# Attention feeding a routed expert layer: logits in a scores' bank, the second routing round drawn forward and partly on GpSimd, expert 0's rows and weights in another order, loads three steps ahead

## The chip, the cores and the metric

The kernel runs on one core of a Trainium2 chip. The metric is the device time of one execution in microseconds (us). Five engines work beside each other, each with its own instruction queue, taken in order: TensorE (PE in the profile; its weight loads are PEld), VectorE (DVE), ScalarE (ACT), GpSimd (POOL) and SyncE (SP), which here issues the plain DMAs. GpSimd issues the indirect ones (gathers and scatters of rows).

## The reference

First a recurrent attention over 4 batches, 8 heads, 768 positions, head size 64; then a layer of 8 experts in which each of the 3072 rows goes to one expert only.

```python
state = gamma[None, :, None, None] * state + einsum('bhd,bhe->bhde', k[:, :, t], v[:, :, t])
y[:, :, t] = scale * einsum('bhd,bhde->bhe', q[:, :, t], state)      # for t in range(768)
x = y.transpose(0, 2, 1, 3).reshape(3072, 512)
logits = x @ w_gate                                                   # 512 x 8
expert_idx = argmax(logits, axis=1)
gate_w = softmax(logits)[arange(3072), expert_idx]
for e in range(8):                                                    # rows sorted by expert
    y_sorted[lo:hi] = maximum(x_sorted[lo:hi] @ w1[e], 0.0) @ w2[e]   # 512x1024, 1024x512
out = gate_w[:, None] * y_sorted[inv_perm]
```

## The kernel before

**Attention** runs in 12 steps (`STEPS`), each a block of 128 positions of two batches and all 8 heads. The recurrence is done in chunks: inside a block by scores (`scores`, L520) under a causal mask (`am`, DVE, L522) and their product with v (`within`, L569); between blocks by a state of 64x64 per head (`with_state` L540, `next_state` L553). k, v and q lie in DRAM with 64 numbers (256 bytes) to a row, q in pieces of two rows. `load` issues them on SP two steps ahead of their use; `scale_q` and `scale_v` multiply by decay factors on GpSimd (L477, L482); `turn_k` and `turn_q` transpose through PE and copy back on ACT (L488, L507, L501).

`within` leaves the block of x transposed in `x[s]`. One step later `logits` (L598) multiplies it by the gate's weights `wg` into the PSUM tile `parts`, ACT copies that to `lgT` (L601), `logits_of` turns it into the PSUM tile `lgp` (L607), and DVE reduces that into `lg` (L608). `to_rows` (DVE, L582) and `store` (SP, L589) write the same block as rows into the DRAM tensor `x_d`.

PSUM has 8 banks: four under the tag `sc` (scores, transposes of q), two under `tr` (transposes of k, state update, `parts`, `lgp`, the routing's small products), two under `y`.

**Routing** (`place`) is a generator, so that its pieces can be put between pieces of the attention. It runs in three rounds over steps 0 to 4, 5 to 8 and 9 to 11 (`NEXT = (0, 5, 9, 12)`). A round finds each row's expert and gate, the row's rank in its expert (`rk`, PE), the pieces of the gate in bf16 (`told`), a one-hot of places (`val`) and of ranks (`here`), multiplies the two (`found`, PE, L687) and adds the result to the table `inv` (L691). After the second round the first 256 rows of experts 0 and 1 are known, and four gathers on GpSimd (L169) fetch them from `x_d` into `xs2`. The places of the pieces in a step are written out by hand in `WHEN`: a letter stands for a point of the step (p, a, b, c), each letter takes the generator to its next `yield`.

**After the last step** the early rows of expert 0, copied from `xs2` to `xe` (DVE, L803), are transposed (`tre`, L821) and copied to `xTa`. Layer 1 of expert 0 on these 256 rows (`layer1`, L226, eight blocks `f`) runs while the third round of the routing is made. Then come the gathers of the later rows, sums and differences of blocks of w2 and of hidden values (`halves_of_w` L268, `halves_of_h` L256 to L259), and `pair` (L352), which makes layer 2 of 256 rows by seven block products instead of eight. The rest of expert 0 and experts 1 to 7 follow in a loop over experts. The weights of expert 0 are loaded within the last steps of the attention (L153 w1, L158 w2), 2 MB each; those of expert 1 need buffers that are free only once the attention's buffers are given up.

From `tc.manual_schedule` on, every engine takes its instructions in the order of the program text. This is true of SP too: a store that waits for DVE holds up the loads behind it.

Of the kernel before, what the change touches and what calls it, by code (L numbers as in the profile page):

```python
# [53 lines left out]
def kernel(  # L54
# [93 lines left out]
    w1v = w1.rearrange("e (dt p) f -> p e dt f", p=P)  # L148
    w2v = w2.rearrange("e (ft p) d -> p e ft d", p=P)

    def weights1(pool, e):
        w1t = pool.tile([P, 1, DT, F], F32, tag="w1t", name="w1t")
        nc.sync.dma_start(w1t, w1v[:, ds(e, 1), :, :])  # L153
        return w1t

    def weights2(pool, e):
# [282 lines left out]
    with ExitStack() as actx:  # L439
# [19 lines left out]
        def load(nm, s, b, parts=1):  # L459
            m, b1, e = where[s]  # L460
            src = {"q": q, "k": k, "v": v}[nm]
            if nm == "q":
                to = att.tile([P, H, 2 * D], F32, tag=nm, name=nm, bufs=3)
                for part in (ts(i, H // parts) for i in range(parts)):
                    nc.sync.dma_start(to[:, part, :], src[2 * b1 + b, part, ts(m, 2 * P), :].rearrange(
                        "h (t e) d -> t h (e d)", e=2))
            else:
                to = att.tile([P, H, D], F32, tag=nm, name=nm, bufs=6)
                nc.sync.dma_start(to, src[2 * b1 + b, :, ts(2 * m + e, P), :].rearrange("h t d -> t h d"))
            raw[nm, s, b] = to  # L470

# [120 lines left out]
        early = []  # L592

        def logits(s):
            parts = ps("tr", 2, "parts")[:, 0 : 2 * P]
            m = P // DT
            for dt in range(DT):
                nc.tensor.matmul(parts[ts(dt, m), :], lhsT=wg[:, dt, :], start=True, stop=True,  # L598
                                 rhs=x[s][:, dt, :, :].rearrange("p b t -> p (b t)"))
            lgT = att.tile([P, 2 * P], F32, tag="lgT", name="lgT", bufs=1)  # L600
            nc.scalar.copy(out=lgT, in_=parts)  # L601
            return lgT

        def logits_of(s, lgT):
            tr = ps("tr", 2, "lgp")[:, 0 : 2 * P].rearrange("p (b t) -> p b t", b=2)
            for b in range(2):
                nc.tensor.transpose(tr[:, b, :], lgT[:, ts(b, P)], ident)  # L607
            return lambda: nc.vector.tensor_reduce(  # L608
                lg[:, 2 * s : 2 * s + 2, :], tr.rearrange("p b (a e) -> p b e a", a=DT)[:, :, 0:E, :], axis=AX.X,
                op=ALU.add)  # L610
# [3 lines left out]
        def place(i):  # L614
# [20 lines left out]
            nc.vector.tensor_reduce(gate, ex, axis=AX.X, op=ALU.add)  # L635
            nc.vector.tensor_scalar(out=gate, in0=gate, scalar1=1e-9, scalar2=None, op0=ALU.add)
            nc.vector.reciprocal(gate, gate)
            yield
            rk = ps("tr", 2, "rk")[:, 0 : n * E].rearrange("p (b e) -> p b e", e=E)
            nc.tensor.matmul(rk, lhsT=before, rhs=oh, start=True, stop=False)  # L640
# [12 lines left out]
            if i == 0:  # L653
# [5 lines left out]
            nc.vector.tensor_tensor(out=at, in0=inner(oh, TC), op=ALU.mult, in1=bass.AP(  # L659
                tensor=is_col.tensor, offset=is_col.offset,  # L660
                ap=[list(is_col.ap[0]), list(is_col.ap[1]), [0, E], list(is_col.ap[2])]))
            if i < NR - 1:
                yield
            part = gate
            for j in range(2, 5):
                nc.vector.tensor_copy(told[:, mine, j], part)
                if j < 4:
                    less = att.tile([P, MOST_T], F32, tag="less", name="less", bufs=2)[:, 0:n]
                    nc.vector.tensor_tensor(out=less, in0=part, in1=told[:, mine, j], op=ALU.subtract)
                    part = less  # L670
            if i < NR - 1:
# [8 lines left out]
            here = small("here", P, dt=BF16)  # L680
            for b in range(n):
                nc.vector.tensor_scalar(out=here[:, b, :], in0=rrow, scalar1=prow[:, b : b + 1], scalar2=None,
                                        op0=ALU.is_equal)
            yield
            found = ps("tr", 2, "found")[:, 0 : 5 * E * TC]
            for b in range(n):
# [31 lines left out]
        load_all("k", 1)  # L718
        load_all("v", 1)
        load("q", 2, 0)  # L720
        ctx.enter_context(tc.manual_schedule(engines={PE, ACT, POOL, DVE, SP}))
        nc.sync.dma_start(wg[:, :, 0:E], w_gate.rearrange("(dt p) e -> p dt e", p=P))
        xTa = first.tile([P, DT, EARLY], F32, tag="xTa", name="xTa")
# [11 lines left out]
        am.append(scores(0, 1))  # L735
        xe = keep.tile([P, HALF, DM], F32, tag="xe", name="xe")
        rest = iter(())
        WHEN = {5: "abc", 6: "ab", 7: "ab", 8: "pa", 9: "ac", 10: "ab", 11: "pa"}

        def step(s, at):  # L740
            if at in WHEN.get(s, ""):
                next(rest, None)

        for s in range(STEPS):
            if s + 2 < STEPS:
                if s % 2 == 0:
                    load("q", s + 2, 1)
                load_all("k", s + 2)
                load_all("v", s + 2)
                if s % 2 and s + 3 < STEPS:  # L750
                    load("q", s + 3, 0)
            if s % 2 and s + 1 < STEPS:
                scale_q(s + 1, 1)
# [12 lines left out]

            def ahead():
                for b in range(2):
                    turn_k(s + 1, b)

            def ahead_q():
                if s % 2:
                    for b in range(2):
                        turn_q(s + 1, b)

            if s:
                lgT = logits(s - 1)
                if s + 1 < STEPS:
                    ahead()
                reduce = logits_of(s - 1, lgT)  # L780
# [16 lines left out]
                if s + 1 < STEPS:  # L797
                    step(s, "a")
            next_state(s)
            step(s, "b")  # L800
            if s + 1 == STEPS:
                for t in range(HALF):
                    nc.vector.tensor_copy(xe[:, t, :].rearrange("p (a q l) -> p q a l", q=Q, l=L),  # L803
                                          xs2[0][:, t, :].rearrange("p (q a l) -> p q a l", q=Q, l=L))
# [9 lines left out]
        we = [att.tile([P, FH * DH], F32, tag=tag, name="we", bufs=bufs)  # L814
              for tag, bufs in (("q", 3), ("q", 3), ("q", 3), ("qs", 2))]
# [29 lines left out]
        S = halves_of_h(hTa, [att.tile([P, FH * P], F32, tag="k", name="he", bufs=6) for _ in range(4)], nc.gpsimd)  # L845
        which = regs(0)

        late = turns(xs2[0], xTa, range(HALF, TC))
# [1 line left out]
        def some(n):  # L850
            for _ in range(n):
                next(late)

        pair(hTa, wa[1], S, T, oa, egates, lambda: fetch_ahead(which, 0),
             lambda name: att.tile([P, FH * P], F32, tag="v", name=name, bufs=6)[:, 0:DH], some,
             (("sc", 4), ("sc", 4), ("y", 2), ("y", 2)))
        scatter(oa, targets(*early, "_e"), range(HALF))
        turn(xs2[1], xT1, range(TC))
# [208 lines left out]
```

## Time and profile before

| what | us |
|---|---|
| median of 3 runs | 471.01 (470.87 to 472.51) |
| the profiled execution, its own time | 471.93 |
| its span, first to last instruction | 470.2 |
| PE busy | 437.0 (93% of the span) |
| DVE busy | 283.9 (60%) |
| GpSimd busy | 245.3 (52%) |
| ACT busy | 127.1 (27%) |
| mean granted TensorE clock | 0.976 |

The attention takes up about the first 120 us of the span, the early rows of expert 0 run to 168 us, the loop over experts takes the rest. The page cuts the span into 40 slices of 11.75 us; a digit is the busy share of a slice in tenths. In the row of the clock a 9 is full speed. In a timeline row the first number is the start, the second the time, and the bracket says how long the engine had been idle and who ended it. In the chain of waits each row is a piece of the path that ended last.

### The profile page before, as it was taken

How to read it: one execution, taken by the hardware profiler on the slowest of the kernel's cores; microseconds unless marked ns; L12 is line 12 of the kernel's file. 1: busy time of each engine (PE TensorE's matmuls, PEld its weight loads, DVE VectorE, ACT ScalarE, POOL GpSimd, SP SyncE). 2: the span in 40 equal slices, each digit the busy share in tenths (PEclk: the TensorE clock that was granted, in tenths of full speed). 3: DMA queues.
4: the chain of work that ended last, by engine and by line, in shares of the span. 5: the costliest groups of instructions: out<-in, count | busy, mean ns of one | idle time of the engine just before them, and what ended most of it. 6: DMA issues, size and time to landing. Idle time of an engine off the chain costs nothing.

```text
span 470.2 us, 9505 instructions
## 1 busy us (share of the span) xinstructions
PE 437.0 (93%) x3595; PEld 355.7 (76%) x3595; DVE 283.9 (60%) x597; ACT 127.1 (27%) x283; POOL 245.3 (52%) x192
## 2 busy tenths in 40 slices
PE   7799989999389799999999999999999999999992
PEld 5678877887277594557996896799799689689772
DVE  4444578769347795762676477568856768754410
ACT  2354444463111020221231123123213212212310
POOL 4565426431302336918851983688198369369311
PEclk9999999999769899999999999999999999999997
DMA  9999989999820049904815360462453416001001
GB/s 203 207 227 241 204 187 255 238 211 310 288 45 18 24 157 393 372 10 183 256 55 182 90 234 4 181 219 100 184 199 116 172 36 231 5 6 62 4 28 49
DMA packets 93927, 72.75 MB, mean 155 GB/s; under 512 B 53866, under 2 KB 78442, under 8 KB 93808
## 3 DMA queue, kind: packets, MB, share of 16 engines
q1 hardware_dynamic: 88544, 58.74, 44.4%
q0 software_dynamic: 5120, 12.60, 7.5%
q8 instruction: 47, 0.77, 0.7%
q14 instruction: 72, 0.59, 0.4%
q10 hardware_dynamic: 144, 0.05, 0.0%
HBM read 60.88 MB, written 14.68 MB: 161 GB/s over the span
## 4 chain that ended last, share of the span: by engine, by line
PE 78%; DMA 6%; DVE 6%; issue 5%; ACT 2%; SPq 1%; POOL 1%; POOLq 0%; ACTq 0%; DVEq 0%
PE p L306 24%; PE p L352 16%; PE p L239 12%; PE p L226 6%; PE sc L520 3%; PE y L569 3%; PE hp L226 3%; PE yp L352 3%; DMA k<-in_k_dram 3%; PE trq L488 2%; PE new L553 2%; ACT kT L507 1%; DMA q<-in_q_dram 1%; PE y L540 1%; DMA xs<-x_d,src_e 1%
## 5 line engine op out<-in xcount | busy, mean ns | idle before, releaser
L239 PE MATMUL p<-w2t,hT 128*8 128x128 f32 (+6 forms) x496 | 66.4, 360 | 0.0
L239 PEld LDWEIGHTS p<-w2t,hT 128*8 128x8 f32 (+6 forms) x496 | 32.6, 123 | 29.5 <-issue 26.8
L212 DVE STREAM_TRANSPOSE xT<-xs 32x512 f32<-32x512 f32 x64 | 44.9, 702 | 6.0 <-issue 4.9
L169 POOL DMA_INDIRECT xs<-x_d,src x28 | 29.3, 1046 | 35.1 <-DVE gate_e L204 23.8
L397 POOL DMA_INDIRECT out_dram<-o,dst x30 | 29.8, 995 | 27.9 <-ACT o L247 11.3
L482 POOL TENSOR_TENSOR vs<-v,dec 128x512 f32<-128x512 f32 x23 | 24.1, 1064 | 35.6 <-DMA v<-in_v_dram 29.7
L522 DVE TENSOR_TENSOR am<-sc,causal 128x512 f32<-128x512 f32 x48 | 29.9, 684 | 19.5 <-PE sc L520 19.4
L212 DVE STREAM_TRANSPOSE xTs<-xs 32x512 f32<-32x512 f32 x48 | 33.7, 702 | 12.7 <-issue 11.9
L1026 POOL COPY turn_of<-t 128x1 f32<-128x1 f32 x6 | 1.1, 182 | 72.5 <-DVE t L292 72.5
L352 PE MATMUL p<-ws,hs 128*128 128x256 f32 x168 | 37.4, 379 | 0.0
L306 PE MATMUL p<-t,s 128*128 128x196 f32 (+5 forms) x192 | 35.8, 329 | 0.0
L306 PE MATMUL p<-t,w1t 128*128 128x196 f32 (+5 forms) x192 | 35.8, 329 | 0.0
L352 PEld LDWEIGHTS p<-ws,hs 128*128 128x128 f32 x168 | 31.9, 190 | 4.3
L310 DVE TENSOR_TENSOR hT<-p,q 128x196 f32<-128x196 f32 (+5 forms) x72 | 24.8, 361 | 15.7 <-PE p L306 15.2
L268 POOL TENSOR_TENSOR ws<-w2t,ws 128x1024 f32<-128x1024 f32 x14 | 33.5, 2391 | 0.6
L268 POOL TENSOR_TENSOR ws<-w2t 128x1024 f32<-128x1024 f32 x14 | 33.1, 2367 | 0.1
L477 POOL TENSOR_TENSOR qs<-q,dec 128x512 f32<-128x512 f32 x22 | 22.6, 1050 | 20.2 <-DMA q<-in_q_dram 17.4
L306 PEld LDWEIGHTS p<-t,s 128*128 128x128 f32 x192 | 32.4, 190 | 0.0
L306 PEld LDWEIGHTS p<-t,w1t 128*128 128x128 f32 x192 | 32.4, 190 | 0.0
L358 DVE SCALAR_TENSOR_TENSOR o<-p,gate,q 128x256 f32<-128x256 f32 x21 | 10.0, 483 | 29.5 <-PE p L352 29.1
L310 DVE TENSOR_TENSOR q<-p,q 128x196 f32<-128x196 f32 (+5 forms) x48 | 16.5, 360 | 17.9 <-PE p L306 12.9
L352 PE MATMUL p<-w2t,hT 128*128 128x256 f32 x112 | 27.0, 382 | 0.2 <-ACT q L367 0.2
(204 smaller groups left out, 828.3 us busy)
## 6 DMA issues: line engine op xcount, KB each, us to landing
w1t<-in_moe_w_dram SPq DMA_DIRECT2D x8, 2048.0 KB, 9.1
w2t<-in_moe_w_dram SPq DMA_DIRECT2D x8, 2048.0 KB, 11.2
k<-in_k_dram SPq DMA_DIRECT2D x24, 256.0 KB, 5.3
v<-in_v_dram SPq DMA_DIRECT2D x24, 256.0 KB, 5.5
x_d<-xg SPq DMA_DIRECT2D x48, 128.0 KB, 3.8
q<-in_q_dram SPq DMA_DIRECT2D x11, 512.0 KB, 6.0
q<-in_q_dram SPq DMA_DIRECT2D x2, 256.0 KB, 3.5
out_dram<-o,dst POOLq DMA_INDIRECT x30, 3.1
```

The lines of the kernel that those rows point to most:

```text
L169: nc.gpsimd.indirect_dma_start(out=xs[:, t, :], out_offset=None, in_=x_d[0:rows, :], in_offset=bass.IndirectOffsetOnAxis(ap=idx[:, t : t + ...
L212: nc.vector.transpose(xT[ts(g, L), :, 0 : n * P].rearrange("p a (t r i) -> p r t a i", r=Q, i=L)[:, r, :, :, :], xs[ts(r, L), tiles[0] : t ...
L226: nc.tensor.matmul(hp, lhsT=w1t[:, 0, dt, ts(f, P)], rhs=xT[:, dt, 0:n], start=(dt == 0), stop=(dt == DT - 1))
L239: nc.tensor.matmul(y[j * z : j * z + m, 0:c], lhsT=hT[:, f, t * P + r0 : t * P + r0 + m], rhs=w2t[:, 0, f, ts(j, c)], start=(i == 0), stop ...
L268: by.tensor_tensor(out=ws[i], in0=sums[i][0], in1=sums[i][1], op=ALU.subtract)
L306: nc.tensor.matmul(rows(y), lhsT=a(d, f), rhs=b(d), start=start and d == 0, stop=d == 1, skip_group_check=True)
L310: nc.vector.tensor_tensor(out=to, in0=rows(y), in1=rows(plus), op=ALU.add)
L352: nc.tensor.matmul(y, lhsT=a[:, f, :], rhs=b[:, f, :], start=start and f == 0, stop=f == FH - 1, skip_group_check=True)
L397: done = nc.gpsimd.indirect_dma_start(out=out[:, :], out_offset=bass.IndirectOffsetOnAxis(ap=idx[:, t : t + 1], axis=0), in_=o[:, t, :], i ...
L477: by.tensor_tensor(out=qs[:, e, part, :], in0=got[:, part, ts(e, D)], op=ALU.mult, in1=inner(dec[:, ts(2 * where[s][0] + e, H)][:, part], D))
L482: by.tensor_tensor(out=vs, in0=raw.pop(("v", s, b)), op=ALU.mult, in1=inner(dec[:, ts(NC + 2 * where[s][0] + where[s][2], H)], D))
L522: nc.vector.tensor_tensor(out=am[j], in0=sc[j], in1=middle(causal[:, :], HP), op=ALU.mult)
```

## The change

- `logits` and `logits_of` share one bank of the tag `sc`, in place of two tiles of the tag `tr`.
- Loads run three steps ahead: k, v and both q of step 2 are issued before the small load of `wg`, k and v have 8 buffers for 6, q has 4 for 3.
- In the second and third round the pieces of the gate (`tell`) and the one-hot of ranks (`find`) go to GpSimd. The second round is put in fewer and earlier pieces: at points a and the new r (ahead of `within`) of step 9, and twice at p of step 10. Point p moves ahead of `logits`.
- The copies to `xe` come after `within` of the last step, one on DVE and one on ACT; `pad_ranks` moves into step 10.
- w1 of expert 0 is loaded as two halves, still in step 9; w2 in step 11, after that step's store; the store of step 10 no longer stands behind both.
- After the last step the logits are finished ahead of layer 1, and the third round is cut at `f` 1 and 4 (before: 0, 2 and 5). The third of the four `halves_of_w` goes to GpSimd.

```diff
-    def weights1(pool, e):
+    def weights1(pool, e, parts=1):
-        nc.sync.dma_start(w1t, w1v[:, ds(e, 1), :, :])
+        for part in (ts(i, F // parts) for i in range(parts)):
+            nc.sync.dma_start(w1t[:, :, :, part], w1v[:, ds(e, 1), :, part])
...
         def logits(s):
-            parts = ps("tr", 2, "parts")[:, 0 : 2 * P]
+            bank = ps("sc", 4, "parts")
+            parts = bank[:, 0 : 2 * P]
...
-        def logits_of(s, lgT):
-            tr = ps("tr", 2, "lgp")[:, 0 : 2 * P].rearrange("p (b t) -> p b t", b=2)
+        def logits_of(s, lgT, bank):
+            tr = bank[:, 2 * P : 4 * P].rearrange("p (b t) -> p b t", b=2)
...
             nc.vector.reciprocal(gate, gate)
+            by = nc.gpsimd if i else nc.vector
+            def tell():
+                part = gate
+                for j in range(2, 5):
+                    by.tensor_copy(told[:, mine, j], part)
+                    if j < 4:
+                        less = att.tile([P, MOST_T], F32, tag="less", name="less", bufs=2)[:, 0:n]
+                        by.tensor_tensor(out=less, in0=part, in1=told[:, mine, j], op=ALU.subtract)
+                        part = less
+            if i:
+                tell()
             yield
...
-            if i < NR - 1:
+            here = small("here", P, dt=BF16)
+            def find():
+                for b in range(n):
+                    by.tensor_scalar(out=here[:, b, :], in0=rrow, scalar1=prow[:, b : b + 1], scalar2=None,
+                                     op0=ALU.is_equal)
+            if i:
+                find()
+            else:
                 yield
...
         load("q", 2, 0)
+        load("q", 2, 1)
+        load_all("k", 2)
+        load_all("v", 2)
         ctx.enter_context(tc.manual_schedule(engines={PE, ACT, POOL, DVE, SP}))
         nc.sync.dma_start(wg[:, :, 0:E], w_gate.rearrange("(dt p) e -> p dt e", p=P))
...
-        WHEN = {5: "abc", 6: "ab", 7: "ab", 8: "pa", 9: "ac", 10: "ab", 11: "pa"}
+        WHEN = {5: "abc", 6: "ab", 7: "ab", 8: "pa", 9: "ar", 10: "pp"}
...
-            if s + 2 < STEPS:
-                if s % 2 == 0:
-                    load("q", s + 2, 1)
-                load_all("k", s + 2)
-                load_all("v", s + 2)
-                if s % 2 and s + 3 < STEPS:
-                    load("q", s + 3, 0)
+            if s + 3 < STEPS:
+                if s % 2:
+                    load_all("q", s + 3)
+                load_all("k", s + 3)
+                load_all("v", s + 3)
...
+            step(s, "p")
             if s:
-                lgT = logits(s - 1)
+                logit = logits(s - 1)
...
-                step(s, "p")
-                if s + 1 == STEPS:
-                    step(s, "a")
                 to_rows(s - 1)
                 reduce()
-                if s - 1 != NEXT[NR - 1]:
-                    store(s - 1)
+                store(s - 1)
                 if s == NEXT[NR - 1]:
-                    wa = [weights1(first, 0)]
-                if s == NEXT[NR - 1] + 1:
+                    wa = [weights1(first, 0, 2)]
+                if s + 1 == STEPS:
                     wa.append(weights2(first, 0))
-                    store(s - 1)
...
             step(s, "b")
-            if s + 1 == STEPS:
-                for t in range(HALF):
-                    nc.vector.tensor_copy(xe[:, t, :]..., xs2[0][:, t, :]...)
+            if s == NEXT[NR - 1] + 1:
+                pad_ranks(acc[:, NR - 1, 0:2])
+            step(s, "r")
             within(s, y, am)
...
+        for t in range(HALF):
+            copy = nc.scalar.copy if t else nc.vector.tensor_copy
+            copy(out=xe[:, t, :]..., in_=xs2[0][:, t, :]...)
-        lgT = logits(STEPS - 1)
+        logit = logits(STEPS - 1)
         rest = place(NR - 1)
-        pad_ranks(acc[:, NR - 1, 0:2])
...
+        logits_of(STEPS - 1, *logit)()
+        next(rest)
         to_rows(STEPS - 1)
         store(STEPS - 1)
         for f in range(FT):
             layer1(EARLY, xTa, wa[0], hTa, f, (("sc", 4),))
-            if f == 0:
-                logits_of(STEPS - 1, lgT)()
-                next(rest)
-            if f == 2:
+            if f == 1:
                 next(rest)
                 ne = count()
-            if f == 5:
+            if f == 4:
                 next(rest)
                 next(rest, None)
...
-        T = halves_of_w(wa[1], we)
+        halves_of_w(wa[1], we, [0, 1])
+        halves_of_w(wa[1], we, [2], nc.gpsimd)
+        T = halves_of_w(wa[1], we, [3])
```

More of the change, by code (lines that the diff above doesn't have):

```diff
@@ L462, in load @@
             if nm == "q":
-                to = att.tile([P, H, 2 * D], F32, tag=nm, name=nm, bufs=3)
+                to = att.tile([P, H, 2 * D], F32, tag=nm, name=nm, bufs=4)
                 for part in (ts(i, H // parts) for i in range(parts)):
@@ L467, in load @@
             else:
-                to = att.tile([P, H, D], F32, tag=nm, name=nm, bufs=6)
+                to = att.tile([P, H, D], F32, tag=nm, name=nm, bufs=8)
                 nc.sync.dma_start(to, src[2 * b1 + b, :, ts(2 * m + e, P), :].rearrange("h t d -> t h d"))
@@ L601, in logits @@
             nc.scalar.copy(out=lgT, in_=parts)
-            return lgT
-        def logits_of(s, lgT):
-            tr = ps("tr", 2, "lgp")[:, 0 : 2 * P].rearrange("p (b t) -> p b t", b=2)
+            return lgT, bank
+        def logits_of(s, lgT, bank):
+            tr = bank[:, 2 * P : 4 * P].rearrange("p (b t) -> p b t", b=2)
             for b in range(2):
@@ L661, in place @@
                 ap=[list(is_col.ap[0]), list(is_col.ap[1]), [0, E], list(is_col.ap[2])]))
-            if i < NR - 1:
-                yield
[L664 to L671, printed above, removed]
+            here = small("here", P, dt=BF16)
[6 more added lines that the diff above has]
+            else:
+                yield
+                tell()
                 yield
@@ L679, in place @@
                 yield
[L680 to L683, printed above, removed]
+                find()
             yield
@@ L737 @@
         rest = iter(())
-        WHEN = {5: "abc", 6: "ab", 7: "ab", 8: "pa", 9: "ac", 10: "ab", 11: "pa"}
+        WHEN = {5: "abc", 6: "ab", 7: "ab", 8: "pa", 9: "ar", 10: "pp"}
         def step(s, at):
-            if at in WHEN.get(s, ""):
+            for _ in range(WHEN.get(s, "").count(at)):
                 next(rest, None)
         for s in range(STEPS):
-            if s + 2 < STEPS:
-                if s % 2 == 0:
-                    load("q", s + 2, 1)
-                load_all("k", s + 2)
-                load_all("v", s + 2)
-                if s % 2 and s + 3 < STEPS:
-                    load("q", s + 3, 0)
+            if s + 3 < STEPS:
[3 more added lines that the diff above has]
+                load_all("v", s + 3)
             if s % 2 and s + 1 < STEPS:
@@ L774, in ahead_q @@
                         turn_q(s + 1, b)
+            step(s, "p")
             if s:
-                lgT = logits(s - 1)
+                logit = logits(s - 1)
                 if s + 1 < STEPS:
                     ahead()
-                reduce = logits_of(s - 1, lgT)
+                reduce = logits_of(s - 1, *logit)
                 if s + 1 < STEPS:
                     ahead_q()
-                step(s, "p")
-                if s + 1 == STEPS:
-                    step(s, "a")
                 to_rows(s - 1)
                 reduce()
-                if s - 1 != NEXT[NR - 1]:
-                    store(s - 1)
+                store(s - 1)
                 if s == NEXT[NR - 1]:
-                    wa = [weights1(first, 0)]
-                if s == NEXT[NR - 1] + 1:
+                    wa = [weights1(first, 0, 2)]
+                if s + 1 == STEPS:
                     wa.append(weights2(first, 0))
-                    store(s - 1)
                 if s in NEXT:
                     rest = chain(rest, place(NEXT.index(s) - 1))
-                if s + 1 < STEPS:
-                    step(s, "a")
+                step(s, "a")
             next_state(s)
             step(s, "b")
-            if s + 1 == STEPS:
-                for t in range(HALF):
-                    nc.vector.tensor_copy(xe[:, t, :].rearrange("p (a q l) -> p q a l", q=Q, l=L),
-                                          xs2[0][:, t, :].rearrange("p (q a l) -> p q a l", q=Q, l=L))
+            if s == NEXT[NR - 1] + 1:
+                pad_ranks(acc[:, NR - 1, 0:2])
+            step(s, "r")
             within(s, y, am)
@@ L808 @@
             step(s, "c")
-        lgT = logits(STEPS - 1)
+        for t in range(HALF):
+            copy = nc.scalar.copy if t else nc.vector.tensor_copy
+            copy(out=xe[:, t, :].rearrange("p (a q l) -> p q a l", q=Q, l=L),
+                 in_=xs2[0][:, t, :].rearrange("p (q a l) -> p q a l", q=Q, l=L))
+        logit = logits(STEPS - 1)
         rest = place(NR - 1)
-        pad_ranks(acc[:, NR - 1, 0:2])
         oa = xs2[0][:, 0:HALF, :]
         we = [att.tile([P, FH * DH], F32, tag=tag, name="we", bufs=bufs)
-              for tag, bufs in (("q", 3), ("q", 3), ("q", 3), ("qs", 2))]
+              for tag, bufs in [("q", 4)] * 4]
         for t in range(HALF):
@@ L843 @@
         arm, over = arms(ne)
-        T = halves_of_w(wa[1], we)
-        S = halves_of_h(hTa, [att.tile([P, FH * P], F32, tag="k", name="he", bufs=6) for _ in range(4)], nc.gpsimd)
+        halves_of_w(wa[1], we, [0, 1])
+        halves_of_w(wa[1], we, [2], nc.gpsimd)
+        T = halves_of_w(wa[1], we, [3])
+        S = halves_of_h(hTa, [att.tile([P, FH * P], F32, tag="k", name="he", bufs=8) for _ in range(4)], nc.gpsimd)
         which = regs(0)
@@ L854 @@
         pair(hTa, wa[1], S, T, oa, egates, lambda: fetch_ahead(which, 0),
-             lambda name: att.tile([P, FH * P], F32, tag="v", name=name, bufs=6)[:, 0:DH], some,
+             lambda name: att.tile([P, FH * P], F32, tag="v", name=name, bufs=8)[:, 0:DH], some,
              (("sc", 4), ("sc", 4), ("y", 2), ("y", 2)))
```

## The prediction

> **What bounds the kernel now.** I read the slices first, then the chain of waits where PE has a hole, then the timeline there. PE is busy in nine tenths of nearly every slice, so the time is PE's work plus PE's holes.
>
> ```profile
> PE   7799989999389799999999999999999999999992
> PEclk9999999999769899999999999999999999999997
> DMA  9999989999820049904815360462453416001001
> ```
>
> The holes are in slices 0, 1, 10, 11 and 13; the granted clock falls with the big one. Its chain of waits (start, us, what):
>
> ```profile
> 121.18 5.62 DMA xs<-x_d,src_e
> 126.83 0.43 DVE xe L803
> 127.28 0.69 DVE xT L575
> 128.02 1.07 PE parts L598 x4
> ```
>
> PE stands from 120.64 to 128.02, 7.4 us. It waits for a copy of x (L575) that has nothing to do with the gathers; in DVE's queue it stands behind the copies to `xe`, and those wait for rows gathered late, since the second round's result came at 119.4. A second hole stands ahead of `pair`, timeline of PE and POOL:
>
> ```profile
> 150.83 1.96 PE L352 MATMUL yp<-w2t,hTa 128*128 128x256 f32 x8 [0.29 <-issue]
> 156.20 7.27 PE L352 MATMUL yp<-we,he 128*128 128x256 f32 x24 [3.40 <-DVE he L257]
> 156.20 1.26 POOL L258 TENSOR_TENSOR he<-hTa,he 128x512 f32<-128x512 f32 x1 [1.74 <-DVE he L257]
> 157.43 1.26 POOL L259 TENSOR_TENSOR he<-hTa 128x512 f32<-128x512 f32 x1
> ```
>
> The third place is small now and matters for what follows, SP and PE in steps 0 and 1:
>
> ```profile
> 14.37 1.04 SPq L722 DMA_DIRECT2D wg<-in_moe_w_gate_dram  x1
> 15.50 2.62 SPq L465 DMA_DIRECT2D q<-in_q_dram  x1
> 18.17 2.11 SPq L469 DMA_DIRECT2D k<-in_k_dram  x2
> 20.32 2.91 SPq L469 DMA_DIRECT2D v<-in_v_dram  x2
> 21.65 0.64 PE L598 MATMUL parts<-xT,wg 128*32 128x256 f32 x8
> 23.67 0.63 PE L488 MATMUL trk<-ident,k 128*128 128x128 f32 x4 [1.38 <-DMA k<-in_k_dram]
> 24.84 0.63 PE L488 MATMUL trk<-ident,k 128*128 128x128 f32 x4 [0.54 <-DMA k<-in_k_dram]
> ```
>
> The gate's weights `wg` are issued ahead of step 2's loads; the first `parts` needs them at 21.65. From 26 to 120 us PE's idle sums to 4.1 us outside the big hole: the attention there is bound by PE, although the DMA engines are at nine tenths too.
>
> **What the Trainium skill says.** "TensorE: Matmul & The Clock Gate", Part 1: the clock is halved after an idle window of some 3.4 us and restored after a busy one. The trace agrees: 0.50 from 123.3 to 136.9 after the 7.4 us hole, and again from 157.4 to 160.8 after 3.4 us of idleness. "DMA: Bandwidth & Descriptors", Queues, rings and completion order: each DMA engine consumes a ring's descriptors in order. The trace agrees: `wg`, 16 KB, took 6.4 us from issue to landing, behind what was issued before it. "SBUF — State Buffer", two separate sides: GpSimd and a VectorE instruction with two SBUF inputs or in a two-port mode lock each other out for a whole instruction. The trace agrees: while POOL scaled v (62.68 to 64.72) two small DVE steps took 0.80 and 0.93 us where their neighbours take 0.24.
>
> ```profile
> 62.68 2.04 POOL L482 TENSOR_TENSOR vs<-v,dec 128x512 f32<-128x512 f32 x2 [2.64 <-DMA v<-in_v_dram]
> 63.02 0.80 DVE L626 TENSOR_TENSOR dl<-lg,mx 128x80 f32<-128x80 f32 x1
> 63.85 0.93 DVE L628 TENSOR_SCALAR top<-dl 128x80 f32<-128x80 f32 x1
> 64.82 0.24 DVE L629 TENSOR_TENSOR top<-top,em 128x80 f32<-128x80 f32 x1
> ```
>
> **The change part by part**, on the clock of the profile before; shifts are summed at the end.
>
> *Loads further ahead.* q, k and v of step 2 (four k/v loads and one q, 1.57 MB) now stand before `wg`. Their issues took from 15.50 to 23.23, 7.7 us, so `wg` is issued at 22.1 instead of 14.37. Landing: it landed at 14.37 + 6.4 = 20.8; q and k then passed in 4.1 us (the last k at 24.84), v needs another 2.4 (two loads at the 1.2 between the two k): 27.2. Issue plus 6.4 gives 28.5. I take 27.6. PE is in order, so the transposes of k and q behind `parts` wait too. With `parts` 0.6 and the k transposes 1.2, `lgp` starts at 29.4 instead of 25.30: +4.1 (bounds: 0 if `wg` overtakes, 5.0). PE is idle for 5.9 us, so I expect half clock when it resumes: one or two windows of 3.4 us, in which half the work gets done, 1.7 to 3.4 lost, up to 6 if transposes don't count as activity; I take 3.0 (bounds 0 and 6). Early loss 7.1. In return k of step 6 is in time: −1.25 (PE's wait at 60.35). POOL's waits for v (29.7 us in 9) end too, worth nothing, since PE hardly ever waits for POOL there.
>
> *Logits in a scores' bank.* In each step `lgp` starts 0.12 us after the last k transpose (a `tr` bank is still being copied), and the state update 0.27 to 0.41 late in four even steps: together about 2.6. With three tiles a step in `tr` for five this goes; I take −2.2. The new wait is `parts` for the first `am`: in step 2 that ends near 32.07, `parts` starts at 32.17; nothing, by a hair (worst 0.1 a step). The fourth q transpose needs a bank too, one is copied by then.
>
> *Second round.* `rk` (0.4) moves ahead of `within` in step 9; the one-hot it reads was ready at 102.93, PE is there at 102.1: +0.9, and `within` is queued behind it. `found` moves ahead of `logits` in steps 8 and 10 and holds a `tr` bank, so the second k transpose waits for one copy: +0.6. On POOL: `find`, 8 instructions of 128 elements. The nearest row is an affine select of 128 (0.28); a memset of 128 takes 0.19, a two-input 512 takes 1.05. I take 0.30, 2.4 in all, from 105.2, and `val` (1.48) shares the lock: 109.1, while PE is there at 108.5 or a bit later: +0.3. `tell`, 5 small ones of some 0.2, is hidden. The four gathers follow at about 112 (0.3 + 1.0 each, behind two scalings of v), when w1, issued near 107, is almost in; the first two land by 119, needed at 121.
>
> *After the last step.* The copy L575 no longer waits: PE goes on at 120.9 with `parts`, transposes from 121.4 (1.2 at full clock, 1.97 before), `lgp` 0.45, the copy to `xTa` to 123.25. Layer 1 starts at 123.3 instead of 132.10: −8.8. Layer 1 to `pair`: before 150.83 − 132.10 = 18.7, of which 2.3 lost to the half clock and 0.45 `lgp`; after 8 x 1.72 + `rk` 0.35 + wait and count 1.1 + `found` 0.6 = 15.9: −2.8. POOL's 6 `find` (1.8) and DVE's `val` (1.16) end near 131.6, `found` is due at 133.5. Then `src` at 135.5, gates and arms to 137.3, three `halves_of_w` on DVE (1.23 each) to 141.0, the two sums L256, L257. On POOL four gathers until 141.2, then the third `halves_of_w`, 2.37 by its L268 rows, against DVE in the same lock, then 2 x 1.26: the third product can start at 147.4, and five products of 1.72 end at 156.1. From the start of `pair` (139.2) that is 16.9, before 168.48 − 150.83 = 17.65; a half-clock window in it costs about what it did. I take −0.3 (bounds −2.1 and +1.0). w2 is issued near 121, lands in some 11, used at 137; w1's second DMA costs SP one more 0.47 issue. From `pair` on everything is relative to its end, expert 1's loads too.
>
> **Sum**: 4.1 + 3.0 − 1.25 − 2.2 + 1.8 − 8.8 − 2.8 − 0.3 = −6.45. The span 470.2 becomes 463.8. The profiled execution took 471.93, 1.7 more than its span and 0.9 more than the median 471.01; off the median: 464.5.
>
> **Rivals.** (1) *The early stall is cheap*: `wg` lands early or the clock stays up or returns at once (−3 to −5), and `pair` goes without the lock (−1.8). For it: a stall of 1.9 us at the same place cost no clock. Against: 5.9 is longer than 3.4. 457.5. (2) *It is dear*: two more half-clock windows (+3), `found` late by one; 468. (3) *The copies still wait*: gathers took 6.1 us to land beside the weights; if the same congestion meets them, PE waits some 3 at 121: 467.5. (4) *Slower*: `find` on POOL. Each us of its price costs 8 at the first `found` and 6 at the second. Past 0.3, time is lost as 14 x (price − 0.3) less a slack of 2.2 at the second; the gain is gone at about 0.9 and past 1.1 the kernel is measurably slower; at 1.3 it takes 476.3. Against: no one-input row of POOL of this size is above 0.28.
>
> **How the numbers follow.** Forecast 0.55, (1) 0.27, (2) 0.09, (3) 0.05, (4) 0.04. The forecast's own range is 461 to 467.5. 80% takes in nearly all of (1) and most of (2): 456 to 469. A difference within 0.5% (2.35 us) is about what a measurement of this kernel can't tell from none; faster is under 468.65: 0.54 + 0.27 and parts of (2) and (3), 0.86; same 0.09; slower 0.05.
>
> **What would show it.** Right: PE's wait for L575 gone, gathers of `src_e` near 112 plus the shift, a wait of PE at the first `parts` for `wg` of about 6 us with the clock at half after it, no PE wait for k later, layer 1 of `xTa` near 127. Wrong: no wait for `wg`; `tre` waiting for `xe`; `found` waiting for `here`; the loop over experts of another length than 302 us (from 168.5 to the end).

## The result, and the profile after

The changed kernel takes 469.31 us (median of 20 runs, 467.27 to 471.92), beside 472.00 for the kernel before on the same chip (20 runs, 469.73 to 476.66). The ratio is **0.9941 [0.9919, 0.9962]**: 2.8 us faster, where 6.5 were forecast. Its profiled execution took 469.96 us over a span of 468.2; mean clock 0.978.

The three rows of slices, now 11.7 us each (busy tenths of PE, granted clock, DMA):

```profile
PE   7779999998887999999999999999989999999992
PEclk9979999998999799999999999999999999999998
DMA  8999999996671079705804441380472416001001
```

The slice of 3 (the tenth, counted from 0) is gone from PE's row, and slices 9 to 12 show a long shallow dent of 8 and 7 in its place. The clock falls in slice 2 (23 to 35 us: after the wait for `wg`), a little in slice 9 (105 to 117: step 10) and in slice 13 (from 152: `pair`). The chain of waits where PE stood for 7.4 us before, and now stands for 0.84:

```profile
124.82 1.92 PE y L570 x32
...
126.76 0.59 ACT xT L578
...
127.38 0.69 DVE xT L576
...
128.11 0.63 PE parts L600 x4
128.74 1.04 PE tre L833 x8
...
130.44 2.64 PE hp L227 x11
```

What is left is a chain of two copies of x^T, on ACT and then on DVE. Layer 1 starts at 130.44 (132.10 before). The timeline of SP and PE where `wg` now stands behind the loads of step 2:

```profile
20.11 2.53 SPq L470 DMA_DIRECT2D v<-in_v_dram  x2
22.75 1.00 SPq L739 DMA_DIRECT2D wg<-in_moe_w_gate_dram  x1
26.60 1.08 PE L600 MATMUL parts<-xT,wg 128*32 128x256 f32 x8 [4.63 <-DMA wg<-in_moe_w_gate_dram]
27.61 1.97 PE L489 MATMUL trk<-ident,k 128*128 128x128 f32 x8
```

`wg` is issued at 22.75 instead of 14.37, PE waits 4.63 us for it and goes on at half clock: `parts` takes 1.08 instead of 0.64, the transposes 1.97 instead of 1.09. No wait for k follows. The timeline of DVE, POOL and PE in step 10 is the new one:

```profile
105.77 0.19 DVE L672 TENSOR_SCALAR prow<-ranks 128x8 int32<-128x8 int32 x1
106.28 0.33 POOL L645 CAST told<-less 128x8 bf16<-128x8 f32 x1
106.58 5.65 POOL L681 TENSOR_SCALAR here<-rrow,prow 128x128 bf16<-128x128 bf16 x8
106.65 1.64 DVE L692 TENSOR_TENSOR val<-at,told 128x1280 bf16<-128x1280 f32 x1
108.73 0.33 PE L701 MATMUL found<-val,here 128*128 128x160 bf16 x2
109.39 0.24 PE L701 MATMUL found<-val,here 128*128 128x160 bf16 x1 [0.34 <-POOL here L681]
...
112.29 0.24 PE L701 MATMUL found<-val,here 128*128 128x160 bf16 x1 [0.34 <-POOL here L681]
112.46 0.64 PE L600 MATMUL parts<-xT,wg 128*32 128x256 f32 x8
```

PE takes one product of `found` each 0.58 us, as POOL hands out one row of the one-hot after another, from 108.73 to 112.46: 3.73 us for work of 0.7. The first of the eight lasts 1.57, beside `val` on DVE (1.64 here, 1.48 before); the rest come 0.58 apart. By windows, the time after it (columns: PE busy, PEld, DVE, ACT, POOL, with instructions; then granted clock, DMA share, GB/s):

```profile
109.00:113.00 4.00, 1.98 (x15) 0.73 (x14) 2.08 (x5) 0.00 (x0) 4.00 (x7) 1.00 0.92 348
113.00:117.00 4.00, 4.00 (x47) 3.57 (x43) 2.98 (x7) 1.55 (x3) 2.98 (x4) 0.57 0.07 19
```

PE half idle for 4 us, then half clock for nearly 4 more. Last, the timeline of POOL, DVE and PE ahead of `pair`:

```profile
147.65 2.43 POOL L269 TENSOR_TENSOR we<-w2t 128x1024 f32<-128x1024 f32 x1
147.80 2.83 DVE L257 TENSOR_TENSOR he<-hTa 128x512 f32<-128x512 f32 x1
151.50 8.46 PE L353 MATMUL yp<-we,he 128*128 128x256 f32 x24 [3.47 <-DVE he L258]
```

Beside POOL's third `halves_of_w` DVE's sum L257 takes 2.83 us instead of 0.69. PE waits 3.47, as long as before (3.40), and three products take 8.46 instead of 7.27: more of the half clock.

By stretches, in us against the kernel before (c1 is an experiment below). Each number is a difference of start times of PE's rows in two profiles; `pair` runs to the end of its last product. The forecast's 0.6 for a k transpose that waits, given for steps 8 and 10 together, is counted in the row of steps 8 and 9.

| stretch | forecast | changed kernel | c1 |
|---|---|---|---|
| start to the scores of step 2 | +7.1 | +5.06 | +4.74 |
| steps 2 to 7 | −3.45 | −4.28 | −3.18 |
| steps 8 and 9 | +1.5 | +0.59 | +0.59 |
| step 10 | +0.3 | **+4.56** | +1.45 |
| step 11 to layer 1 | −8.8 | −7.59 | −8.83 |
| layer 1 | −2.8 | −3.03 | −3.03 |
| `pair` | −0.3 | +1.19 | −1.42 |
| loop over experts | 0 | +1.5 | +1.1 |
| sum | −6.45 | −2.0 | −8.6 |

One term is off by 4.3 us and decides: step 10. The others are off by up to 2.0 each, in both directions, and by 0.2 in sum; that they cancel is luck.

### The profile page after: what moved, and what is told of

It is laid out like the page before. It is cut to its first block, busy times and chain, and to the rows that moved or that the text cites. A ratio compares the mean times of both kernels' runs of the same rounds, so it can differ in the third digit from the quotient of the medians.

```text
span 468.2 us, 9505 instructions
## 1 busy us (share of the span) xinstructions
PE 437.6 (93%) x3595; PEld 358.8 (77%) x3595; DVE 277.4 (59%) x571; ACT 125.2 (27%) x284; POOL 258.0 (55%) x217
## 4 chain that ended last, share of the span: by engine, by line
PE 78%; DVE 7%; DMA 4%; SPq 3%; issue 2%; POOL 2%; ACT 1%; POOLq 0%; DVEq 0%; ACTq 0%
PE p L307 24%; PE p L353 18%; PE p L240 13%; PE p L227 5%; PE y L570 3%; PE sc L521 3%; DMA q<-in_q_dram 3%; DVE xT L213 2%; SPq L470 2%; PE new L554 2%; PE trk L489 2%; PE hp L227 2%; PE yp L353 1%; PE y L541 1%; PE parts L600 1%
## 5 line engine op out<-in xcount | busy, mean ns | idle before, releaser
L311 DVE TENSOR_TENSOR hT<-p,q 128x196 f32<-128x196 f32 (+5 forms) x72 | 23.8, 359 | 19.4 <-PE p L307 18.5
L359 DVE SCALAR_TENSOR_TENSOR o<-p,gate,q 128x256 f32<-128x256 f32 x21 | 10.1, 483 | 30.9 <-PE p L353 30.4
L521 PE MATMUL sc<-qT,kT 64*128 64x128 f32 x384 | 25.6, 280 | 2.5 <-ACT kT L508 2.3
```

What stands on the lines that cost most here:

```text
L311: nc.vector.tensor_tensor(out=to, in0=rows(y), in1=rows(plus), op=ALU.add)
L521: nc.tensor.matmul(sc[j][:, a, :], lhsT=kT[r, a, :], rhs=qT[r, a, :], start=True, stop=True)
```

## Experiments

Every kernel was timed against the kernel before on its own chip. The medians of before there are 469.1 to 470.7, so ratios are compared; 0.01 is 4.7 us. "Below the changed kernel" is a difference of two such ratios, turned into us.

**The theory**: POOL's price for the one-hot, 0.58 us where 0.30 was assumed, lies on PE's path in step 10 and brings a half-clock window with it. **Rivals**: the order of the pieces is at fault, whoever makes the one-hot; the loss lies elsewhere (the late `wg`, the lock ahead of `pair`).

### e1: wg ahead of step 2's loads

```diff
-        load("q", 2, 1)
-        load_all("k", 2)
-        load_all("v", 2)
...
         nc.sync.dma_start(wg[:, :, 0:E], w_gate.rearrange("(dt p) e -> p dt e", p=P))
+        load("q", 2, 1)
+        load_all("k", 2)
+        load_all("v", 2)
```

> The changed kernel with the load of wg put back in its old place, ahead of the second q, the k and the v of step 2; the lead of three steps stays. Theory (wg's place in SP's queue costs the early 5 us): PE's wait of 4.6 us for wg and the half clock after it are gone, the scores of step 2 start near 30.3 instead of 35.25 as in the kernel before, a wait of some 1.9 us for k of step 2 is back, and all later work moves up: about -4.9 us. Rival A (the longer lead itself crowds the DMA engines, so that k or q is late wherever wg stands): PE waits as long for k or q, gain under 1 us. Rival B (the early loss is made good later, because loads get ahead while PE stands): PE waits for k in steps 3 to 8, gain 0 to 2 us.

459.96 us, ratio 0.9813 [0.9794, 0.9832]: 6.0 us below the changed kernel. The scores of step 2 start at 29.09 instead of 35.25; step 10 still takes 13.2 us. The waits for k of step 2 are back (0.84 and 0.46). The longer lead needs no late `wg`. This is the largest gain of any one line here, but its cost had been forecast, at 7.1; it explains no miss.

### b1: only the late wg, in the kernel before

```diff
-        nc.sync.dma_start(wg[:, :, 0:E], w_gate.rearrange("(dt p) e -> p dt e", p=P))
...
                 load_all("v", s + 2)
+                if s == 0:
+                    nc.sync.dma_start(wg[:, :, 0:E], w_gate.rearrange("(dt p) e -> p dt e", p=P))
```

> The kernel before, with one edit: the load of wg stands behind q, k and v of step 2 in SP's queue; loads stay two steps ahead. Theory (the place of wg is a loss of its own): PE waits 4 to 5 us for wg at the first parts, half clock follows, the scores of step 2 start 5 us later (before: 30.19), and the time is 5 us above before, ratio 1.009 to 1.012. Rival (the attention is bound by its loads, which only change places, so the stall is made up by step 8): the scores of step 8 start within 1.5 us of before's 85.81 and the ratio is 1.000 to 1.004.

476.85 us, ratio 1.0137 [1.0088, 1.0187], 6.4 us dearer. PE's timeline:

```profile
26.07 1.08 PE L598 MATMUL parts<-xT,wg 128*32 128x256 f32 x8 [4.48 <-DMA wg<-in_moe_w_gate_dram]
```

The scores of step 2 start 5.1 later than before (35.31), those of step 8 still 4.2 later (90.00). Little of the stall is made up.

### a3: the same wait for wg with PE kept busy

```diff
             step(s, "p")
+            if s == 1:
+                for _ in range(5):
+                    warm(512)
```

> The changed kernel with five dummy products of 128x512 (0.86 us each at full clock, result unused) on PE ahead of the parts of step 1, where PE stands 4.6 us for wg. The wait itself stays. Theory (the early loss of 5 us is 3.5 of waiting and 1.5 to 2 of half clock after it): the clock stays at 1.00 from 24 to 32 us, the scores of step 2 start at 33.3 to 33.8 (35.25 in the changed kernel, 30.19 before), ratio 0.989 to 0.992. Rival (the loss is all waiting, or the window falls elsewhere): 35 and 0.993 to 0.996; if wg lands early and the products stand in the way, 36 or more.

464.54 us, ratio 0.9894 [0.9866, 0.9923], 2.2 below the changed kernel. By windows (same columns as above) and on PE's timeline:

```profile
24.00:28.00 4.00, 4.00 (x26) 2.11 (x25) 0.00 (x0) 0.94 (x3) 3.17 (x3) 1.00 0.99 207
28.00:32.00 4.00, 4.00 (x74) 3.83 (x74) 0.92 (x2) 2.90 (x7) 0.66 (x1) 1.00 1.03 253
26.11 0.64 PE L600 MATMUL parts<-xT,wg 128*32 128x256 f32 x8
32.50 2.06 PE L521 MATMUL sc<-qT,kT 64*128 64x128 f32 x32
```

The changed kernel had clocks of 0.57 and 0.58 in these two windows. `parts` starts at 26.11, 0.49 earlier than in the changed kernel, and the scores of step 2 come 2.75 earlier, more than expected. So of the early 5.06 us some 2.3 are half clock and 2.8 waiting. How much the half clock takes varies: in six other profiles with the same text up to there (a1, a2, c1, e2, e3, e7) these scores start at 33.57 to 35.02, so 5.06 is the dearest case of seven. The "Trainium skill", page "TensorE: Matmul & The Clock Gate", Part 1, says that the clock is set by how busy PE has been of late. This run agrees, and the products that kept it up were of no use to the result.

### b2: only the scores' bank, in the kernel before

```diff
-            parts = ps("tr", 2, "parts")[:, 0 : 2 * P]
+            bank = ps("sc", 4, "parts")
+            parts = bank[:, 0 : 2 * P]
...
-            tr = ps("tr", 2, "lgp")[:, 0 : 2 * P].rearrange("p (b t) -> p b t", b=2)
+            tr = bank[:, 2 * P : 4 * P].rearrange("p (b t) -> p b t", b=2)
```

> The kernel before, with one edit: parts and lgp share one bank of the tag sc. Theory (the banks of the tag tr were what PE waited for): from the scores of step 2 to those of step 8, 55.6 us before, 2.2 less, the time 2 to 4 us below before, ratio 0.991 to 0.996. Rival (the gain in steps 2 to 8 of the changed kernel came from the longer lead of the loads): the stretch shortens by less than 0.8 and the ratio is 0.998 to 1.001; or the new wait of parts for am takes it back.

467.27 us, ratio 0.9956 [0.9936, 0.9977], 2.1 us, the expected size; but the stretch from step 2 to step 8, 55.75 us, did not shrink in its profile. Steps 2 to 4 took 24.2 instead of 25.9, steps 6 and 7 17.6 instead of 18.4, and step 5 gave it back, 13.9 instead of 11.3:

```profile
58.90 0.66 PE L488 MATMUL trk<-ident,k 128*128 128x128 f32 x4 [1.75 <-DMA k<-in_k_dram]
59.96 0.66 PE L488 MATMUL trk<-ident,k 128*128 128x128 f32 x4 [0.41 <-DMA k<-in_k_dram]
```

PE came to k of step 6 sooner than the load did, and half clock followed (mean 0.88 in the step). In this stretch the bank's gain needs k in time, which the forecast's two separate terms, −2.2 and −1.25, did not say; the longer lead without the bank was not run. Steps 8 to 10 took 1.7 less than before in this profile (25.49 against 27.19), so the bank does pay where k is not late.

### a1: copies to xe back ahead of within

```diff
             step(s, "r")
+            if s + 1 == STEPS:
+                for t in range(HALF):
+                    copy = nc.scalar.copy if t else nc.vector.tensor_copy
+                    copy(out=xe[:, t, :]..., in_=xs2[0][:, t, :]...)
             within(s, y, am)
...
-        for t in range(HALF):
-            copy = nc.scalar.copy if t else nc.vector.tensor_copy
-            copy(out=xe[:, t, :]..., in_=xs2[0][:, t, :]...)
```

> The changed kernel with the two copies to xe put back ahead of within of step 11, as before. The gathers there are issued from 115 us, 4.7 earlier than before. Theory (PE's 7.4 us hole ended because the rows are gathered earlier; the place of the copies no longer matters): the copies find their rows there, PE has no wait over 1 us between within and layer 1, time as the changed kernel, ratio to before 0.992 to 0.996. Rival (the order of the copies was what ended it, as the prediction had it): the hole is back with 2 us or more, ratio 0.998 or above.

467.90 us, ratio 0.9938 [0.9913, 0.9963], as the changed kernel. DVE's timeline has the copy with no wait for its rows:

```profile
125.97 0.42 DVE L816 COPY xe<-xs 128x512 f32<-128x512 f32 x1
```

Before, the gathers were issued 6.7 us after the start of step 11's scores (119.66 and 113.00), here 3.9 before it (115.51 and 119.44). With the rows gathered this early the hole stays closed without the new place of the copies. The forecast had counted on both; whether the place would have closed it alone, no run shows.

### e2: the one-hot on DVE

```diff
-                    by.tensor_scalar(out=here[:, b, :], in0=rrow, scalar1=prow[:, b : b + 1], scalar2=None,
+                    nc.vector.tensor_scalar(out=here[:, b, :], in0=rrow, scalar1=prow[:, b : b + 1], scalar2=None,
```

> The changed kernel with the one-hot of ranks (find) of rounds two and three on DVE instead of GpSimd, everything else in place. Theory (the price of find on GpSimd, 0.70 us each by the trace, is what holds found in step 10): found becomes one run of 0.8 us instead of 3.9 with gaps, the clock stays up in step 10, the scores of step 11 start 4.6 less 0.7 (DVE must now do find ahead of val) earlier: about -3.6 us. Rival (val or the DVE queue holds found, and GpSimd only hides it): found starts some 3 us late all the same, gain under 1 us.

466.66 us, ratio 0.9944 [0.9923, 0.9965]: the gain did not come. The theory in this simple form fell. The timeline of POOL, DVE and PE (of an execution that took 470.67 us, above this kernel's median, so its times are read here for what waits for what):

```profile
105.16 2.05 POOL L483 TENSOR_TENSOR vs<-v,dec 128x512 f32<-128x512 f32 x2
105.07 3.01 DVE L681 TENSOR_SCALAR here<-rrow,prow 128x128 bf16<-128x128 bf16 x8
108.00 1.48 DVE L692 TENSOR_TENSOR val<-at,told 128x1280 bf16<-128x1280 f32 x1
109.53 0.71 PE L701 MATMUL found<-val,here 128*128 128x160 bf16 x8 [2.11 <-DVE val L692]
```

With POOL freed, the scaling of v for step 11 moves up beside the one-hot, and DVE's eight take 3.01 us where they take 1.39 alone. A wait for `val` took the place of the wait for `here`. The new theory: POOL's price was replaced by POOL's lock.

### e7: the one-hot on DVE, and the scaling of v out of its way

```diff
-                    by.tensor_scalar(out=here[:, b, :], in0=rrow, scalar1=prow[:, b : b + 1], scalar2=None,
+                    nc.vector.tensor_scalar(out=here[:, b, :], in0=rrow, scalar1=prow[:, b : b + 1], scalar2=None,
...
-            if s + 1 < STEPS:
+            if s + 1 < STEPS and s not in (10,):
                 for b in range(2):
                     scale_v(s + 1, b)
...
+            if s in (10,):
+                for b in range(2):
+                    scale_v(s + 1, b, nc.vector)
             next_state(s)
```

> The changed kernel with the one-hot of ranks on DVE in all rounds, and the two scalings of v for step 11 on DVE, behind the pieces of the routing, instead of on POOL beside them. Theory (on DVE the one-hot lost what it gained to the scaling of v, which holds the shared port): the eight take 1.4 us on DVE instead of 3.0, found waits less than 0.5 us for val, step 10 takes 9 to 10 us instead of 13.2 in the changed kernel and 14.3 with the one-hot on DVE alone; ratio to before 0.984 to 0.988. Rival (step 10 is long because the second round is too early in it, whoever makes the one-hot): step 10 stays above 12 us and the ratio is 0.993 to 0.996. A third way: the scaling on DVE (two of some 0.6 us) itself delays the logits or am: step 10 between, ratio 0.989 to 0.992.

463.78 us, ratio 0.9866 [0.9825, 0.9907], 3.5 us below the changed kernel. DVE's and PE's timeline:

```profile
105.63 1.39 DVE L681 TENSOR_SCALAR here<-rrow,prow 128x128 bf16<-128x128 bf16 x8
106.93 1.49 DVE L692 TENSOR_TENSOR val<-at,told 128x1280 bf16<-128x1280 f32 x1
108.47 0.71 PE L701 MATMUL found<-val,here 128*128 128x160 bf16 x8 [0.49 <-DVE val L692]
```

`found` waits 0.49, the clock stays up, step 10 takes 10.1 us instead of 13.2. The order of the pieces is the same, so that rival falls, and the lock is what e2 met. The scaling of v by itself is not the cause in the changed kernel: it starts there at 112.20, behind the eight. The "Trainium skill", page "SBUF — State Buffer", two separate sides, says that of a GpSimd instruction and a DVE one with two SBUF inputs or in a two-port mode, whichever starts first holds the shared pair of ports to its end. No view shows which mode the compare runs in, but 3.01 beside the scaling against 1.39 without it agrees.

### a2: the one-hot made twice on POOL

```diff
-                for b in range(n):
+                for b in list(range(n)) * (2 if i == 1 else 1):
```

> The changed kernel with the one-hot of ranks of round 2 made twice on POOL (16 instructions for 8, same result). Theory (the price of POOL's one-hot lies on the path of step 10): 8 x 0.70 = 5.6 us more until found, step 10 from 13.2 to 18.8 us or up to 2 more with the clock; time 5.6 to 7.6 above the changed kernel, ratio to before 1.006 to 1.011. Rival (the gaps in step 10 come from the order of the pieces or from a lock, not from POOL's price): step 10 grows by less than 2, ratio below 1.000.

471.78 us, ratio 1.0036 [1.0015, 1.0058], 4.5 us above the changed kernel; step 10 takes 18.7 us (+5.5). POOL and PE:

```profile
104.89 10.25 POOL L681 TENSOR_SCALAR here<-rrow,prow 128x128 bf16<-128x128 bf16 x16
111.15 0.31 PE L701 MATMUL found<-val,here 128*128 128x160 bf16 x1 [4.03 <-POOL here L681]
```

16 take 10.25, 8 take 5.65: 4.6 for eight, 0.58 each. The expectation's 0.70 a piece held the lock's 1 us in it, so its 5.6 was too high, and the ratio stays below the 1.006 that it named. But the step grows by the added price and some half clock: the dose lies on the path.

### b3: the one-hot on POOL in the kernel before

```diff
-                nc.vector.tensor_scalar(out=here[:, b, :], in0=rrow, scalar1=prow[:, b : b + 1], scalar2=None,
+                (nc.gpsimd if i else nc.vector).tensor_scalar(out=here[:, b, :], in0=rrow, scalar1=prow[:, b : b + 1], scalar2=None,
```

> The kernel before with one edit: the one-hot of ranks of rounds 2 and 3 on POOL. There POOL is free from 109.4 us on and found comes at 117.5, so 5.6 us fit in ahead of it. Theory (POOL's price costs only where the result is wanted at once): found waits less than 0.5 us in step 11, round 3 costs at most 1 us, ratio 0.998 to 1.003. Rival (the eight on POOL lock DVE wherever they stand): DVE's steps beside them are longer, ratio 1.005 or above.

470.28 us, ratio 0.9987 [0.9965, 1.0009], no change that can be told. POOL and PE:

```profile
108.27 5.94 POOL L682 TENSOR_SCALAR here<-rrow,prow 128x128 bf16<-128x128 bf16 x8
116.03 0.72 PE L687 MATMUL found<-val,here 128*128 128x160 bf16 x8
```

The same dear instructions end at 114.2 and are wanted at 116.0: `found` does not wait. The price counts together with the earlier place.

### e3: all four halves of w on DVE

```diff
-        halves_of_w(wa[1], we, [0, 1])
-        halves_of_w(wa[1], we, [2], nc.gpsimd)
-        T = halves_of_w(wa[1], we, [3])
+        T = halves_of_w(wa[1], we)
```

> The changed kernel with all four halves_of_w on DVE again. Theory (the third on GpSimd holds the shared port for 2.4 us while DVE's first sum of h waits, 2.83 us for 0.69): that sum takes 0.7 again, pair's second product starts about 1.0 us earlier, -0.9 to -1.3 us. Rival (DVE is the bound there, and 1.2 us more on it costs as much): 0 to +0.3 us.

464.46 us, ratio 0.9919 [0.9889, 0.9950]: 1.0 below the changed kernel, within what these intervals leave open. The place itself is clear on PE's and DVE's timeline:

```profile
146.42 0.68 DVE L257 TENSOR_TENSOR he<-hTa 128x512 f32<-128x512 f32 x1
147.97 1.97 PE L353 MATMUL yp<-we,he 128*128 128x256 f32 x8 [2.28 <-DVE he L258]
```

The sum takes 0.68 again, and the second product starts 4.17 us after the first (143.80) instead of 5.36.

### c1: e7 and e3 together, wg still late

> The changed kernel, wg still late, with the two places mended where the forecast was too low: the one-hot of ranks on DVE with the scalings of v for step 11 moved behind the routing's pieces, and all four halves of w on DVE. Theory (the missing 4 us lie in POOL's price at found and in the lock ahead of pair): the forecast's own sum comes true, 6 to 8 us below before, ratio 0.983 to 0.988, with step 10 near 10 us and yb some 4.2 us after the start of pair. Rival (another step of the sum holds the miss, the loop over experts or the clock): 0.990 or above.

462.80 us, ratio 0.9851 [0.9817, 0.9884]: 7.0 us below before, where 0.9862 had been forecast for the change (464.5 to 471.01). PE's timeline:

```profile
110.08 0.71 PE L701 MATMUL found<-val,here 128*128 128x160 bf16 x8 [0.50 <-DVE val L692]
146.68 7.10 PE L353 MATMUL yp<-we,he 128*128 128x256 f32 x24 [2.22 <-DVE he L258]
```

With two places mended the forecast's sum comes out, but this is no clean test of it: the lock ahead of `pair` was part of the forecast. e7, where only the one-hot's place is mended, already has the forecast ratio (0.9866), and the terms that are left in it are off in both directions. c1's column in the table adds up to 8.6, more than 7.0, because the profiled execution of before (471.93) is above the median of before on c1's chip (469.27).

### e4, e8, e9: versions that beat both kernels

e4 joins e1, e2 and e3.

> All three edits together: wg first, find on DVE, halves_of_w on DVE. Theory (three separate places on PE's path, none absorbed): the sum, -9 to -10 us against the changed kernel, near 460 us. Rival (slack later takes up part of it, because gathers, w1 or w2 then come late): -5 us or less, with a wait of PE for xe, w1 or w2.

457.64 us, ratio 0.9782 [0.9742, 0.9821], 7.5 below the changed kernel: less than expected, and about what e1, e2 and e3 gave alone (6.9 together). In step 10 the scaling came late enough (104.27) and `found` did not wait; but in step 9 the scaling of v for step 10 locked DVE, `rk` waited 1.52 for `ohs`, and the step took 10.7.

e8 also moves the scalings of v for steps 10 and 11 to DVE, behind the pieces.

```diff
+            if s in (9, 10):
+                for b in range(2):
+                    scale_v(s + 1, b, nc.vector)
             next_state(s)
```

> The three edits together (wg first, one-hot of ranks on DVE, all halves of w on DVE), and the scalings of v for steps 10 and 11 on DVE behind the pieces of the routing instead of on POOL. In the kernel with the three edits step 9 took 10.7 us and PE waited 1.5 there for a DVE that POOL had locked. Theory of the lock: step 9 falls to 9.2, step 10 stays at 9.1, time 1.5 us below the three edits' own, ratio to before 0.973 to 0.976. Rival (DVE has no room for 2.4 us more): 0.978 or above.

457.11 us, **ratio 0.9737 [0.9694, 0.9780]**. Step 9 falls to 9.0; but step 10 rises to 12.3, as the 1.25 us of scaling stand in DVE's queue ahead of `own`, and `found` waits 1.71 for `val`. e9 puts one of those two scalings where DVE waits for ACT's exponential and the other behind the second piece of step 10.

> The three edits together; of the four scalings of v for steps 10 and 11 on DVE one is put where DVE waits for ACT's exponential in step 9, one behind the second piece of the routing in step 10, two behind the logits of step 10. In the version with all of them behind the pieces, the first two held up own by 1.2 us and found waited 1.7 us for val. Theory: found waits 0.6 or less, step 9 stays at 9.1 and step 10 falls from 12.3 to 9.5 or less; ratio to before 0.967 to 0.972. Rival (the wait only passes on to the state update, which needs the scaled v at once): 0.973 or above.

459.11 us, ratio 0.9748 [0.9709, 0.9788]. `found` waits 0.48 and step 10 takes 10.2, but the expected ratio is missed: in its profile the scores of step 2 start at 31.63 instead of e8's 29.25, ahead of anything the edit touches. The three intervals overlap; which is best is open.

## Why the prediction was wrong

**The early stall** was forecast at 4.1 of waiting and 3.0 of half clock; 2.8 and 2.3 were measured (a3). `wg` landed at 26.5, and 27.6 had been taken. This term was 2.0 too dear here, 2.3 to 3.7 in the six other profiles, and helped.

**k in time and the bank** (−3.45 together): −4.28. Right in size. The split was wrong: in b2 the bank's gain is lost at the late k.

**`rk` and `found`** (+1.5): +0.59; `rk` waited 0.15 for `ohs`, where 0.9 had been forecast.

**`find` on POOL** (+0.3) is the step that failed. Its price of 0.30 came from the nearest one-input row, an affine select of 128; the eight came 0.58 apart, on DVE 0.17. PE took `found` row by row and was about 3.0 us late in all. 8 x 0.28, 2.2 us, is the price. Two smaller terms were wrong beside it. `tell` was put down as hidden, but it stands ahead of `find` in POOL's queue: `prow` was ready at 105.96, and `find` started at 106.58, when `tell` ended. And PE came to `found` about half a us sooner than forecast, since `rk` hardly waited. The lock with `val` was foreseen, and was less than forecast (1.0 for 1.48). The second part of the miss is that no half clock was counted: after the dent the clock was 0.57 for 4 us, and `trk`, `parts` and `new` took 1.76, 0.64 and 1.84 where step 9 shows 1.09, 0.38 and 1.15, so 1.6 more. 3.0 and 1.6 make the 4.6 measured; `found`'s own 0.7, new in this step, and the bank's gain of about as much cancel. No run kept PE busy in this wait, so the 1.6 is read from durations and not tested by itself. Rival 4 named this mechanism, and `found` waiting for `here` was among the forecast's own signs of being wrong. But its formula takes the slack of the second `found` off the cost of the first too: at 0.58 it gives 14 x 0.28 less 2.2, 1.7 us. There was no slack at the first `found`, where 8 x 0.28 alone makes 2.2, and enough at the second, which did not wait: round 3 cost nothing.

**Step 11 to layer 1** (−8.8): −7.59, and −8.83 in c1. The hole is gone, and the earlier gathers are enough for it (a1). The scores of step 11 took 2.93 instead of 2.06 in the changed kernel's profile, with pauses that the profile puts to no wait; a1 and a2 have such pauses too, c1, a3 and e1 have none there. Why is open.

**Layer 1** (−2.8): −3.03, right. The forecast's terms add up to 15.8 us, not to the 15.9 that it gives; 15.7 was measured.

**`pair`** (−0.3): +1.19 here, but the same code took 17.6 to 17.9 us in e1, e7, a3 and a2, 18.6 in a1, and 17.81 before. The difference is the share of half clock, which varies from run to run (three products 7.10 to 8.46). The lock foreseen there costs 1.2 (e3), less than the forecast had allowed for (1.8, by its rival 1).

**The loop over experts** (0): 300.4 to 303.3 us in the profiles of this study, e2's aside; before 301.6. The +1.5 lies within this spread; no effect of the change is shown.

## What to carry to other kernels

A piece of work that is given to another engine needs a price on that engine from a row of the same operation; where there is none, take a high bound when PE is to consume the result at once. Price and place go together: the same eight instructions cost nothing that can be told with 8 us ahead of them, and made their step 4.3 us longer than forecast where the result was wanted at once, some two thirds through the wait and one third through the clock that falls after it. Before relieving POOL, ask what it will do with the time: the next thing in its queue came up beside DVE's work, which took 3.01 us in place of 1.39 and left no gain.

## What the runs showed of the hardware that was not expected

- A compare of 128 bf16 elements with a per-partition number takes 0.58 us on GpSimd, start to start, and 0.17 on VectorE. The "Trainium skill", page "GPSIMD Engine Reference", 4.1, calls one-input work there roughly line-rate; for this operation the measurement decides: 3.4 times slower.
- PE need not stop for long for the clock to fall. After the changed kernel's 4 us of 50% busy (109 to 113), with no wait over 0.34 us, the clock was 0.57 for the next 4 us. In e7, after 4 us of 69% busy at the same place (108 to 112), it stayed at 1.00. Where between the two the limit lies is open.
- Five products whose result nobody uses, put into a wait of 4.6 us, took 2.2 us off the whole time (a3).
